# Attention, a gated layer and eight experts in one kernel: steps in pairs over three batches, loads in a set order, routing in one run

## The chip, the cores and the metric

One core of one Trainium2 chip. A core has five engines that run side by side and meet at semaphores: TensorE (PE, matmuls), VectorE (DVE), ScalarE (ACT), GpSimd (POOL) and SyncE (SP, which here issues loads and stores). Transfers run on 16 DMA engines. The metric is the device time of one execution in microseconds (us).

## The reference, cut to what matters

```python
# attention: 4 batches, 8 heads, 576 positions, head size 64; float32
scores = q @ k.T / 8                      # heads 0-3: the last 32 positions
scores = where(mask, scores, -1e9)        # heads 4-7: every 32nd position
x = softmax(scores) @ v                   # -> x: 2304 tokens x 512
x = ((x @ w_a) * (x @ w_b)) @ w_out       # w_*: float64, 512 x 1536 and 1536 x 512
logits = x @ w_gate + log1p(exp(x @ w_noise)) * noise
top2 = the two largest of 8 logits; weights = their softmax
for e in range(8):                        # w1[e]: 512 x 1024, w2[e]: 1024 x 512
    out[tokens of e] += weight * (relu(x @ w1[e]) @ w2[e])
```

## The kernel before

Every product of the two layers is made of three fp32r matmuls (`mm3`, lines 186 to 188), high part by high part, high by low, low by high. So every weight and every activation is split into a high part (written by ACT) and a low part (DVE).

**The stages.** `load_m1` reads the float64 weights as pairs of integers in blocks (`raw`, line 158) and turns them into high and low parts with integer work on DVE and two copies on ACT (`split64`, lines 161 to 177; `ct` is its scratch). It is a generator: `conv_to(n)` runs it up to step n. Attention is worked out in units of two heads of a batch (`Unit`), four units a batch in the order `HPS`. A unit has 14 steps on PE: `T` transposes q and k (4 steps, line 247), `Q` makes scores (2 halves x 2 steps, line 277) and ends in `E`, the softmax on DVE and ACT, `P` transposes the probabilities (4 steps, line 318), `PV` multiplies by v (2 steps, line 331; result in `xf`). `att_pipe` puts the steps of neighbouring units into one another and yields after each.

Batch 0 goes first, alone, with the mask added by a matmul (`pemask`, line 268), and its probabilities come from one exponential for each block of columns (line 306). The main loop then takes five chunks c of tokens (four of 512; the last, of 256, holds the 64 last tokens of each batch, taken from `tails`) through 12 blocks f of the hidden layer each: `stage_a(c, f)` makes a * b for 128 hidden columns (`pa`, `pb`, `gh`, `gl`), and `stage_b` adds the block before to the output (`po`). Between halves of these products `point()` is called, six times a block: it advances one step of attention of batch c + 1 (`attq`), and every third time (every second in the last chunk) one step of what is in `bgq`. There stand, taken in turn: `finish(c)` (router logits of a chunk, then `route`: two best experts, their ranks by a matmul at line 470, the slots, and scatters of (token, weight) into `table`, line 496), `clear_out`, the loads of the first expert (`load_expert`) and `fetch` (line 716 loads 128-row tiles of the table, line 722 gathers their rows, `spread` transposes and splits them, lines 731 to 733). In batches 1 to 3 DVE adds the mask while it reads the scores (line 286); batches 2 and 3 use one wide exponential (`wide`).

The experts follow in passes; there `pump()` advances the same queue.

**What sets the order.** Within the main loop PE runs its instructions in the order in which the program writes them (`tc.manual_schedule`). All other engines, PE before and after that loop, and the DMA queue of SP take what a scheduler with modelled durations puts next, earlier lines first. Every engine runs its own list in order: an instruction that waits holds those behind it.

**Places.** q, k and v tiles of batch 0 rotate through six slots, two of which are the staging slots `st0` and `st1`, which batch 1's `ql` and `kl` and later the experts' weights use. Raw blocks have two buffers, and at step k block k + 1 is asked for:

```python
while len(raws) < min(k + 2, len(blocks), 99 if k >= NPAIR else NPAIR):
    raws.append(load_raw(blocks[len(raws)][0], 512 * blocks[len(raws)][2]))
```

Attention steps and router steps in the main loop use two PSUM buffers with the tag `t`, in turn.

Of the kernel before, what the change touches and what calls it, by code (L numbers as in the profile page):

```python
# [32 lines left out]
def attention_moe_kernel(ctx: ExitStack, tc: tile.TileContext, q, k, v, w_a, w_b, w_out,  # L33
# [165 lines left out]
    class Unit:  # L199
# [4 lines left out]
        def __init__(self, tile, bank, b, hp, pemask, wide):  # L204
            self.tile, self.bank, self.b, self.hp, self.pemask, self.wide = tile, bank, b, hp, pemask, wide
# [30 lines left out]
        def T(self, i):  # L236
# [11 lines left out]
            if self.wide and i // 2:  # L248
# [8 lines left out]
        def Q(self, half, x):  # L257
            n, g, m = self.n, self.g, self.m
            msk = maskAB[:, half:half + 3, :] if self.local else maskS[:, None, :].to_broadcast([72, 4, 72])
            if x == 0:  # L260
                self.s[half] = self.tile("s", [n, 2, g, m])
                st = self.tile("sst", [96, 1 if self.wide else 2, 8])
                self.mx, self.sm[half] = st[:n, 0, 0:2 * g], st[:n, 0 if self.wide else 1, 0:2 * g]
# [3 lines left out]
            if self.pemask:  # L267
                nc.tensor.matmul(ps, identb[:n, :n], msk, start=True, stop=False)
            for ii in range(g):
# [4 lines left out]
                else:  # L274
# [3 lines left out]
                                 start=not self.pemask, stop=not self.pemask or ii == g - 1)  # L278
# [12 lines left out]
        def E(self, half):  # L291
            n, g = self.n, self.g
# [3 lines left out]
            if not self.pemask:  # L296
                nc.vector.tensor_reduce(mx, s3, axis=AX.X, op=OP.max)
            if self.wide:
                if not self.pemask:
# [40 lines left out]
    def att_pipe(us, ahead, done=None):  # L340
# [8 lines left out]
        if ahead == 2:  # L349
            us[1].load_v()  # L350
        for n, u in enumerate(us):
# [11 lines left out]
            if last:  # L363
                last.PV(1)
                if done:
                    done(last)
                if n + ahead - 1 < len(us):
                    us[n + ahead - 1].load_v()
# [22 lines left out]
        if done:  # L391
            done(u)
# [38 lines left out]
    def route(c, lg):  # L431
# [7 lines left out]
        yield  # L439
# [14 lines left out]
        yield  # L454
# [10 lines left out]
        nc.vector.tensor_add(ms, oh[:, :, 0, :], oh[:, :, 1, :])  # L465
        yield
# [26 lines left out]
        yield  # L493
        for j in range(J):
# [7 lines left out]
            yield  # L502

    pair = [None]

    def store_x2(c, ps, j):
        if j % 2 == 0:
            pair[0] = rpool.tile([128, 2, DM], F32, name="row", tag=f"row{j // 2}")
        row = pair[0][:, j % 2, :]
# [13 lines left out]
    bgq, attq = [], []  # L523
# [10 lines left out]
    def pump():  # L534
        advance(attq)
        advance(bgq)

    def drain():
        while bgq or attq:
# [22 lines left out]
    def load_m1():  # L562
# [8 lines left out]
        raws = []  # L571
        for k, (_, f, n, i) in enumerate(blocks):
            while len(raws) < min(k + 2, len(blocks), 99 if k >= NPAIR else NPAIR):
                raws.append(load_raw(blocks[len(raws)][0], 512 * blocks[len(raws)][2]))
# [5 lines left out]
    cp = m1.enter_context(tc.tile_pool(name="conv", bufs=1))  # L580
    a1 = ExitStack()
    p1 = a1.enter_context(tc.tile_pool(name="att1", bufs=1, reuse_waits="tile"))
    nraw = [0]

    def next_of(n):
        nraw[0] += 1
        return nraw[0] % n

    conv_room["raw"] = lambda m: cp.tile([128, 1024, 2], I32, name="raw", tag=f"u{next_of(2)}")[:, 0:m, :]
    cts = []  # L590

    def ct_tile(m):

        if not cts:
            ct = cp.tile([128, 2, 1024], I32, name="ct", tag="u2")
            cts.extend((ct[:, 0], ct[:, 1]))
        cts.append(cts.pop(0))
        return cts[-1][:, 0:m]

    conv_room["ct"] = ct_tile  # L600
    conv = load_m1()
    nconv = [0]
# [9 lines left out]
    def p1tile(name, shape):  # L612
        if name in ("ql", "kl", "vl"):
            nslot[0] += 1
            i = nslot[0] % 6
            return stage.tile(shape, F32, name=name, tag=f"st{i}") if i < 2 else \
                p1.tile(shape, F32, name=name, tag=f"qkv{i}")
        return p1.tile(shape, F32, name=name, tag=name, bufs=P1BUFS[name])

# [15 lines left out]
    att = ExitStack()  # L635
    apool = att.enter_context(tc.tile_pool(name="att", bufs=1, side="right", reuse_waits="tile"))
# [7 lines left out]
    def attend(b, wide):  # L644
        us = [Unit(atile, bank1, b, hp, False, wide) for hp in HPS]
        us[0].load_qk()
        us[0].load_v()
        return att_pipe(us, 1)

    attq.append(attend(1, False))  # L650

    def stage_a(c, f, point):
# [4 lines left out]
        def half(tag, w):  # L657
            ps = psum.tile([128, n], F32, name="pa" if tag == "A" else "pb", tag=tag)
            for i, kd in enumerate(HPS):
                mm3(ps, tuple(t[:, kd, cols] for t in w), xT[c, kd], i == 0, i == KD - 1)  # L660
                if i == 1:
                    point()
# [16 lines left out]
    def stage_b(c, f, g, point):  # L679
# [4 lines left out]
        for j in range(J):  # L684
            mm3(po[c][j], tuple(t[:, 128 * j:128 * j + 128] for t in g), w, f == 0, f == NF - 1)
            if 2 * (j + 1) in (J, 2 * J):
                point()
# [15 lines left out]
    xpool = {}  # L703

    def xset(e, g):
        n = 3 if g == 0 else 2
        p = xpool[e % 2, g]
        if (e, g) not in XS:
            t = f"x{g}{e % 2}"
            XS[e, g] = (p.tile([128, KD, 128 * n], F32R, name=t + "h", tag=t + "h"),  # L710
# [9 lines left out]
    def gather(e, t):  # L720
        g = xpool["g"].tile([128, DM], F32, name="g", tag="g", bufs=2)
# [13 lines left out]
    def fetch(e, tiles):  # L735
# [3 lines left out]
        for t in tiles:  # L739
            gs.append((t, gather(e, t)))  # L740
            yield
            if len(gs) == 2:
# [232 lines left out]
```

## Time and profile before

| | us |
|---|---|
| runs | 1170.78, 1167.08, 1170.57; median 1170.57 |
| the profiled execution | 1169.36 |
| its span, first to last instruction | 1167.6 |
| PE busy | 1102.8 (94%) |
| DVE busy | 525.3 (45%) |
| ACT busy | 418.0 (36%) |
| GpSimd busy | 144.0 (12%) |

Shares are of the span. The main loop's first full block starts at about 85 us, the last chunk at 599 us and the first expert's matmuls at 677 us. Matmuls overlap, so spacing between starts tells more of PE's pace than the length of one.

### The profile page before, as it was taken

To read this page: it belongs to the slowest core of one execution; us is meant where nothing else is said; L and a number is where in the kernel's file an instruction comes from. 1 tells how busy PE (TensorE), PEld (TensorE's weight loads), DVE (VectorE), ACT (ScalarE), POOL (GpSimd) and SP (SyncE) were. 2 spreads that over 40 slices of the span, in tenths; PEclk is the share of its full clock that TensorE was granted. 3 is DMA by queue.
4 is the path that set the end of the run, shared out by engine and by line. 5 is a ranking of instruction groups with operands and counts; after the bars stand their busy time and mean duration, and the time that the engine had idled before them with its cause. 6 is when DMAs were issued, how large, how long until landed. Compare 5 with 4: busy or idle time off the path is not lost.

```text
span 1167.6 us, 16084 instructions
## 1 busy us (share of the span) xinstructions
PE 1102.8 (94%) x6381; PEld 927.2 (79%) x6381; DVE 525.3 (45%) x1109; ACT 418.0 (36%) x936; POOL 144.0 (12%) x136
## 2 busy tenths in 40 slices
PE   6768999999999999999999699999999998999996
PEld 5546777777777777888888589988999897988995
DVE  5688985355435465211326361245342434242111
ACT  5666664233223242221225251244242424232111
POOL 0000000000200002000020313231030313021112
PEclk9969999999999999999999999999999999999998
DMA  8544522101111111730013643266253626242023
GB/s 183 176 123 153 177 80 65 61 22 32 37 26 58 31 36 49 268 112 1 1 37 110 127 126 57 46 194 183 78 139 92 156 82 166 66 116 40 11 35 48
DMA packets 88549, 105.02 MB, mean 90 GB/s; under 512 B 43664, under 2 KB 48400, under 8 KB 88464
## 3 DMA queue, kind: packets, MB, share of 16 engines
q1 hardware_dynamic: 78352, 82.89, 23.9%
q0 software_dynamic: 10112, 21.02, 9.9%
q8 instruction: 52, 0.85, 0.3%
q14 instruction: 33, 0.27, 0.1%
HBM read 78.53 MB, written 25.35 MB: 89 GB/s over the span
## 4 chain that ended last, share of the span: by engine, by line
PE 78%; DMA 10%; DVE 7%; issue 2%; POOL 2%; ACT 1%; SPq 1%; DVEq 0%; ACTq 0%; POOLq 0%
PE ph L186 6%; PE ph L187 6%; PE ph L188 6%; PE py L186 6%; PE py L187 6%; PE py L188 5%; PE po L186 4%; PE pb L186 4%; PE pa L186 4%; PE pb L188 4%; PE pb L187 4%; PE po L188 4%; PE po L187 4%; PE pa L187 4%; PE pa L188 4%; DMA st<-in_moe_w_dram 3%
## 5 line engine op out<-in xcount | busy, mean ns | idle before, releaser
L825 DVE SCALAR_TENSOR_TENSOR hl<-ph,hh 128x256 fp32r<-128x256 f32 (+1 forms) x128 | 62.1, 488 | 198.2 <-ACT hh L824 197.9
L824 ACT ACTIVATE hh<-ph 128x256 fp32r<-128x256 f32 (+1 forms) x128 | 55.2, 433 | 208.5 <-PE ph L188 208.5
L671 DVE TENSOR_TENSOR a<-a,pb 128x512 f32<-128x512 f32 (+1 forms) x60 | 37.9, 631 | 129.2 <-PE pb L188 129.2
L496 POOL DMA_INDIRECT table<-pay,sli x36 | 35.7, 992 | 452.7 <-DVE sli L483 424.3
L849 POOL DMA_INDIRECT out_dram<-y,tb x40 | 65.1, 1627 | 193.1 <-ACT y L848 127.0
L666 ACT ACTIVATE a<-pa 128x512 f32<-128x512 f32 (+1 forms) x60 | 33.2, 553 | 110.0 <-PE pa L188 107.5
L672 ACT ACTIVATE gh<-a 128x512 fp32r<-128x512 f32 (+1 forms) x60 | 35.3, 588 | 81.2 <-DVE a L671 80.2
L722 POOL DMA_INDIRECT g<-x,tb x40 | 40.6, 1016 | 183.1 <-PE tt L731 165.4
L673 DVE TENSOR_TENSOR gl<-a,gh 128x512 fp32r<-128x512 f32 (+1 forms) x60 | 38.0, 633 | 16.3 <-ACT gh L672 15.8
L277 PEld LDWEIGHTS tt<-kT,qT 64*72 64x72 f32 (+1 forms) x336 | 30.4, 149 | 18.2 <-issue 14.9
L318 PE MATMUL tt<-ident,s 72*72 72x72 f32 (+1 forms) x224 | 30.9, 263 | 11.9 <-DVE s L310 7.8
L318 PEld LDWEIGHTS tt<-ident,s 72*72 72x72 f32 (+1 forms) x224 | 24.4, 141 | 22.4 <-ACT ct L168 4.5
L319 ACT ACTIVATE pT<-tt 128x288 f32<-128x288 f32 (+1 forms) x64 | 25.8, 409 | 42.0 <-PE tt L318 41.6
L277 PE MATMUL tt<-kT,qT 64*72 64x72 f32 (+1 forms) x336 | 39.1, 253 | 0.7 <-DVE s L286 0.7
L186 PE MATMUL py<-w6h,hh 128*128 128x512 f32 x80 | 33.1, 416 | 6.8 <-ACT hh L824 3.6
L331 PEld LDWEIGHTS tt<-pT,vl 72*64 72x64 f32 (+1 forms) x448 | 22.3, 156 | 18.6 <-issue 8.6
L331 PE MATMUL tt<-pT,vl 72*64 72x72 f32 (+1 forms) x448 | 29.8, 270 | 5.6 <-ACT pT L319 5.6
L731 PE MATMUL tt<-ident,g 128*128 128x128 f32 x160 | 26.0, 281 | 9.5 <-DMA g<-x,tb 8.1
L186 PE MATMUL py<-w2h,hh 128*128 128x512 f32 x80 | 33.2, 415 | 0.6 <-DVE y L846 0.6
L186 PE MATMUL pa<-xh,w0h 128*128 128x512 f32 (+1 forms) x80 | 33.6, 420 | 0.0
L731 PEld LDWEIGHTS tt<-ident,g 128*128 128x128 f32 x160 | 20.6, 145 | 15.1 <-DMA g<-x,tb 7.6
L187 PE MATMUL py<-w6l,hh 128*128 128x512 f32 x80 | 32.6, 407 | 0.0
(288 smaller groups left out, 3307.8 us busy)
## 6 DMA issues: line engine op xcount, KB each, us to landing
st<-in_moe_w_dram SPq DMA_DIRECT2D x64, 512.0 KB
out_dram<-zero SPq DMA_DIRECT2D x13, 512.0 KB
raw<-in_moe_w_a_dram SPq DMA_DIRECT2D x4, 1024.0 KB
raw<-in_moe_w_b_dram SPq DMA_DIRECT2D x4, 1024.0 KB
raw<-in_moe_w_out_dram SPq DMA_DIRECT2D x4, 1024.0 KB
x<-row SPq DMA_DIRECT2D x16, 256.0 KB
vl<-in_v_dram SPq DMA_DIRECT2D x16, 160.0 KB
ql<-in_q_dram SPq DMA_DIRECT2D x16, 144.0 KB
```

Of the source, the lines that this page charges most:

```text
L186: nc.tensor.matmul(ps, w[0], x[0], start=start, stop=False)
L187: nc.tensor.matmul(ps, w[0], x[1], start=False, stop=False)
L188: nc.tensor.matmul(ps, w[1], x[0], start=False, stop=stop)
L277: nc.tensor.matmul(ps[:, ii, :], self.qT[r0:r0 + 64, q0:q0 + n], self.kT[r0:r0 + 64, k0:k0 + m], start=not self.pemask, stop=not self.pema ...
L318: nc.tensor.transpose(ps[:, ii, :], self.s[half][:, x, ii, :], ident[:n, :n])
L331: nc.tensor.matmul(ps[64 * hh:64 * hh + 64, jl, :], self.vl[:, hh, g * half + jl, :], self.pT[:, x, ii, :], start=True, stop=True)
L673: nc.vector.tensor_sub(gl, a, gh.bitcast(F32))
L722: nc.gpsimd.indirect_dma_start(out=g, out_offset=None, in_=x2, in_offset=bass.IndirectOffsetOnAxis(ap=TB[e, t][:, 0:1], axis=0))
L731: nc.tensor.transpose(ps[:, kd, :], g[:, 128 * kd:128 * kd + 128], ident)
L824: nc.scalar.activation(hh, ph, AF.Relu)
L825: nc.vector.scalar_tensor_tensor(hl, ph, 0.0, hh.bitcast(F32), op0=OP.max, op1=OP.subtract)
L849: ins = nc.gpsimd.indirect_dma_start(out=out, out_offset=bass.IndirectOffsetOnAxis(ap=TB[e, t][:, 0:1], axis=0), in_=y, in_offset=None, co ...
```

## The change

- **Batch 0.** All loads of q, k, v are issued first, unit by unit, with the first three raw blocks between them, and SP runs this part in program order. The tiles lie in places of `ring` that weights of block 4 on will use. Raw blocks have three buffers (the third is the place of `row`), and at step k block k + 2 is asked for. In the second half of units 1 to 3 (`wides`) DVE subtracts the maximum from all columns, ACT makes one exponential, DVE the sum.
- **Batches 1 to 3** are one `att_pipe` of 12 units. `may` holds the first `PV` of a batch until the chunk before has given its `xf` places back. In batch 1 (`mask` is "act") PE adds the mask by matmul, as in batch 0, and ACT copies the scores to SBUF.
- **Points.** Three a block instead of six: after `pa`, after `pb`, after `stage_b`. Each advances attention by a step, then `finq` (now the queue of `finish`) or, if that is empty, attention by a second step, then `bgq`, twice in the last chunk.
- **Routing.** `route` runs without a break up to the one-hot sums, gives way three times, then runs from the rank matmul to all scatters.
- **The first fetch** leaves the queue: table and two gathers ahead of block 8 of the last chunk, first `spread` and third gather ahead of block 11, the rest after the last block. `load_expert(0)` starts at block 4, not 5.
- **Experts.** `fetch` gathers three tiles ahead instead of two; the split rows of one set lie in the place of `row`; a chunk's four rows share one tile.

```diff
             if x == 0:
...
             ps = self.bank("Q", [n, g, m])
-            if self.pemask:
+            pemask = self.mask != "dve"
+            if pemask:
                 nc.tensor.matmul(ps, identb[:n, :n], msk, start=True, stop=False)
...
-            if self.pemask:
+            if self.mask == "pe":
                 nc.vector.tensor_reduce(mx, ps, axis=AX.X, op=OP.max)
-                if self.wide:
+                if self.wides[half]:
                     nc.vector.tensor_sub(s[:, x], ps, mx[:, :, None].to_broadcast([n, g, m]))
                 self.src.append(ps)
             else:
-                nc.vector.tensor_add(s[:, x], ps, msk)
+                if pemask:
+                    nc.scalar.activation(s[:, x], ps, AF.Copy)
+                else:
+                    nc.vector.tensor_add(s[:, x], ps, msk)
                 self.src.append(s[:, x])
...
             if nxt and n + 1 + ahead < len(us):
                 us[n + 1 + ahead].load_qk()
+            while not may(u):
+                yield
             u.PV(0)
             yield
...
     def pump():
-        advance(attq)
+        advance(finq)
         advance(bgq)
...
         for k, (_, f, n, i) in enumerate(blocks):
-            while len(raws) < min(k + 2, len(blocks), 99 if k >= NPAIR else NPAIR):
-                raws.append(load_raw(blocks[len(raws)][0], 512 * blocks[len(raws)][2]))
+            ahead(min(k + (3 if k < NPAIR - 2 else 2), 99 if k >= NPAIR else NPAIR))
...
-    us = [Unit(p1tile, bank0, 0, hp, True, False) for hp in HPS]
-    us[0].load_qk()
-    us[1].load_qk()
-    us[0].load_v()
-    for i, _ in enumerate(att_pipe(us, 2, lambda u: split_kd(0, u.hp))):
-        conv_to(min(12, 1 + i * 12 // 50))
-    conv_to(12)
+    us = [Unit(p1tile, bank0, 0, hp, "pe", (False, i > 0)) for i, hp in enumerate(HPS)]
+    with tc.manual_schedule(engines={mybir.EngineType.SP}):
+        for i, u in enumerate(us):
+            u.load_qk()
+            u.load_v()
+            conv_room["ahead"](min(i + 1, 3))
+        for i, _ in enumerate(att_pipe(us, 9, lambda u: split_kd(0, u.hp))):
+            conv_to(min(12, i * 12 // 50))
+        conv_to(12)
...
-    attq.append(attend(1, False))
+    us = [Unit(atile, bank1, b, hp, "act" if b == 1 else "dve", (b > 1,) * 2) for b in range(1, B) for hp in HPS]
+    us[0].load_qk()
+    us[0].load_v()
+    attended = set()
+    may = [1]
+    attq.append(att_pipe(us, 1, lambda u: attended.add((u.b, u.hp)), lambda u: u.b <= may[0]))
...
             def point():
                 npt[0] += 1
                 if c == 0:
-                    conv_to(n0 + (n1 - n0) * ((npt[0] - 1) % 6 + 1) // 6)
+                    conv_to(n0 + (n1 - n0) * ((npt[0] - 1) % 3 + 1) // 3)
                 advance(attq)
-                if npt[0] % (2 if c == NCH - 1 else 3) == 0:
+                advance(finq if finq else attq)
+                advance(bgq)
+                if c == NCH - 1:
                     advance(bgq)
...
-            if (c, f) == (NCH - 1, 5):
+            if (c, f) == (NCH - 1, 4):
                 bgq.append(load_expert(0))
-            if (c, f) == (NCH - 1, 8):
-                bgq.append(fetch(0, [0, 1, 2]))
+            if c == NCH - 1 and f in (8, 11):
+                for _ in range(3 if f == 8 else 2):
+                    next(first)
```

## Rows read from the trace of the kernel before

**Rows 1.** Busy time by window: us, each engine's busy time (count), granted clock, DMA, GB/s.

```profile
5.00:84.00 79.00, 57.91 (x358) 41.99 (x358) 57.23 (x116) 51.01 (x177) 0.00 (x0) 0.91 0.61 159
84.00:180.00 96.00, 91.82 (x524) 70.10 (x525) 83.83 (x133) 58.70 (x151) 0.00 (x0) 0.95 0.48 143
660.00:677.00 17.00, 8.90 (x49) 7.51 (x48) 3.68 (x8) 3.79 (x8) 6.59 (x7) 0.80 0.50 82
```

**Rows 2.** Waits, 0 to 120 us: waiter, releaser, us in total, times, longest.

```profile
ACT ct L168 <- DVE ct L167: 14.5, 9, 4.6
...
PE tt L318 <- DVE s L310: 7.8, 3, 4.1
...
PE tt L331 <- ACT pT L319: 5.6, 5, 2.2
...
PE tt L247 <- DMA ql<-in_q_dram: 3.8, 1, 3.8
...
PE tt L318 <- ACT xf L334: 3.2, 2, 3.0
```

**Rows 3.** Line 158, the raw loads: who waited for them, us and times.

```profile
  DVE ct L167: 19.1, 14
```

**Rows 4.** SyncE's queue, timeline: start, us, instruction.

```profile
80.31 1.26 SPq L218 DMA_DIRECT2D ql<-in_q_dram  x2
```

**Rows 5.** Waits, 596 to 680 us, the last chunk.

```profile
PE tt L731 <- DMA g<-x,tb: 8.1, 2, 7.4
...
DVE pay L486 <- DMA table<-pay,sli: 3.7, 1, 3.7
...
PE tt L426 <- DVE x2T L420: 2.9, 2, 2.1
...
PE po L186 <- ACT gh L672: 1.6, 1, 1.6
```

**Rows 6.** GpSimd, timeline, with the idle time before and its releaser.

```profile
648.82 0.97 POOL L496 DMA_INDIRECT table<-pay,sli  x1 [0.30 <-issue]
659.46 1.28 POOL L496 DMA_INDIRECT table<-pay,sli  x1 [9.67 <-issue]
```

**Rows 7.** SyncE's queue around 655 us.

```profile
655.58 0.34 SPq L716 DMA_DIRECT2D tb<-table  x1
```

**Rows 8.** DVE by line and shape, 0 to 480 us: busy us, mean ns | idle before.

```profile
L286 DVE TENSOR_TENSOR s<-tt,maskAB 96x384 f32<-96x384 f32 x24 | 13.2, 552 | 9.7 <-PE tt L277 9.3
...
L302 DVE TENSOR_REDUCE sst<-s 96x6 f32<-96x768 f32 x8 | 7.6, 947 | 3.1 <-ACT s L301 3.1
```

**Rows 9.** PE, timeline: start us, duration us, instructions.

```profile
8.11 1.17 PE L268 MATMUL sc<-maskAB,identb 96*96 96x384 bf16 x3
...
49.29 0.63 PE L187 MATMUL pa<-xl,w0h 128*128 128x512 f32 x1
49.72 0.63 PE L188 MATMUL pa<-xh,w0l 128*128 128x512 f32 x1
50.14 1.16 PE L247 MATMUL sc<-ident,ql 72*128 72x72 f32 x8
...
103.10 0.42 PE L247 MATMUL tt<-ident,ql 72*128 72x72 f32 x4
103.32 0.48 PE L186 MATMUL po<-w2h,gh 128*128 128x512 f32 x1
103.64 0.39 PE L187 MATMUL po<-w2l,gh 128*128 128x512 f32 x1
103.86 0.39 PE L188 MATMUL po<-w2h,gl 128*128 128x512 f32 x1
```

**Rows 10.** Transfers of the slot table, then of gathered rows.

```profile
DMA to landing us min/median/max: 2.8/3.6/6.7
...
DMA to landing us min/median/max: 3.3/3.4/7.6
```

**Rows 11.** PE's waits among the experts, 676 to 1140 us.

```profile
PE py L186 <- ACT hh L824: 3.6, 1, 3.6
```

More of the change, by code (lines that the diff above doesn't have):

```diff
@@ L199, in attention_moe_kernel, with __init__ @@
     class Unit:
-        def __init__(self, tile, bank, b, hp, pemask, wide):
-            self.tile, self.bank, self.b, self.hp, self.pemask, self.wide = tile, bank, b, hp, pemask, wide
+        def __init__(self, tile, bank, b, hp, mask, wide):
+            self.tile, self.bank, self.b, self.hp, self.mask, self.wides = tile, bank, b, hp, mask, wide
             self.local = hp < 2
@@ L261, in Q @@
                 self.s[half] = self.tile("s", [n, 2, g, m])
-                st = self.tile("sst", [96, 1 if self.wide else 2, 8])
-                self.mx, self.sm[half] = st[:n, 0, 0:2 * g], st[:n, 0 if self.wide else 1, 0:2 * g]
+                wide = self.wides[half]
+                st = self.tile("sst", [96, 2, 8])
+                self.mx, self.sm[half] = st[:n, 0, 0:2 * g], st[:n, 1, 0:2 * g]
                 self.src = []
@@ L291, in E @@
         def E(self, half):
+            wide = self.wides[half]
             n, g = self.n, self.g
@@ L364, in att_pipe @@
                 last.PV(1)
[L365 to L368, printed above, removed]
+                done(last)
+                if ahead == 1:
+                    u.load_v()
                 yield
@@ L501, in route @@
                 scatters.append(ins)
-            yield
-    pair = [None]
+        yield
+    four = [None]
     def store_x2(c, ps, j):
-        if j % 2 == 0:
-            pair[0] = rpool.tile([128, 2, DM], F32, name="row", tag=f"row{j // 2}")
-        row = pair[0][:, j % 2, :]
+        if j == 0:
+            four[0] = rpool.tile([128, 4, DM], F32, name="row", tag="row")
+        row = four[0][:, j, :]
         if j % 2:
@@ L534, in pump @@
     def pump():
-        advance(attq)
+        advance(finq)
         advance(bgq)
     def drain():
-        while bgq or attq:
+        while bgq or finq:
             pump()
@@ L580, in attention_moe_kernel, with raw_tile, halves, get @@
     cp = m1.enter_context(tc.tile_pool(name="conv", bufs=1))
+    att = ExitStack()
+    apool = att.enter_context(tc.tile_pool(name="att", bufs=1, side="right"))
     a1 = ExitStack()
-    p1 = a1.enter_context(tc.tile_pool(name="att1", bufs=1, reuse_waits="tile"))
+    p1 = a1.enter_context(tc.tile_pool(name="att1", bufs=1))
     nraw = [0]
-    def next_of(n):
+    def raw_tile(m):
         nraw[0] += 1
[L587 to L600, printed above, removed]
+        i = nraw[0] % 3
+        return (cp if i else rpool).tile([128, 1024, 2], I32, name="raw", tag=("row", "u0", "u1")[i])[:, 0:m, :]
+    def halves(pool, shape, name, tag):
+        t = []
+        def get(m):
+            if not t:
+                both = pool.tile([shape[0], 2] + shape[1:], I32, name=name, tag=tag)
+                t.extend((both[:, 0], both[:, 1]))
+            t.append(t.pop(0))
+            return t[-1][:, 0:m]
+        return get
+    conv_room["raw"] = raw_tile
+    conv_room["ct"] = halves(cp, [128, 1024], "ct", "u2")
     conv = load_m1()
+    next(conv)
     nconv = [0]
@@ L613, in p1tile, with slot8 @@
         if name in ("ql", "kl", "vl"):
+            i = nslot[0]
             nslot[0] += 1
-            i = nslot[0] % 6
-            return stage.tile(shape, F32, name=name, tag=f"st{i}") if i < 2 else \
-                p1.tile(shape, F32, name=name, tag=f"qkv{i}")
+            return slot8(i, shape)
         return p1.tile(shape, F32, name=name, tag=name, bufs=P1BUFS[name])
+    big = {}
+    def slot8(i, shape):
+        if i // 2 not in big:
+            big[i // 2] = ring.tile([128, 2, 1024], F32, name=f"qkv{i // 2}", tag=f"w{3 + i // 4}{'hl'[i // 2 % 2]}")
+        n = shape[1] * shape[2] * shape[3]
+        return big[i // 2][:shape[0], i % 2, 0:n].rearrange("p (a b c) -> p a b c", a=shape[1], b=shape[2])
     def bank0(name, shape):
@@ L709, in xset @@
             t = f"x{g}{e % 2}"
+            if p is rpool:
+                both = p.tile([128, 2, KD, 128 * n], F32R, name=t, tag="row")
+                XS[e, g] = (both[:, 0], both[:, 1])
+                return XS[e, g]
             XS[e, g] = (p.tile([128, KD, 128 * n], F32R, name=t + "h", tag=t + "h"),
@@ L749, in attention_moe_kernel @@
     with tc.manual_schedule(engines={mybir.EngineType.PE}):
+        first = fetch(0, [0, 1, 2])
         prev = None
@@ L765, in attention_moe_kernel @@
                 last_units(cp, 10, ("u0", "u1", "u2"))
-                conv_room["raw"] = lambda m: rpool.tile([128, 512, 2], I32, name="raw", tag=f"row{next_of(2)}")
+                conv_room["raw"] = halves(rpool, [128, 512, 2], "raw", "row")
                 conv_room["ct"] = lambda m: rpool.tile([128, 512], I32, name="ct", tag="x2T")
             if f == NF - 1:
-                while attq:
+                while c + 1 < B and (c + 1, HPS[-1]) not in attended:
                     advance(attq)
@@ L801, in attention_moe_kernel @@
         last_rows = stage_b(*prev, pump)
+        for _ in first:
+            pass
     m1.close()
```

60 lines of the change are left out of this document (27 added, 33 removed).

## Prediction, made before the changed kernel was run

> **What bounds the kernel now.** I read the page first: TensorE (PE) is busy nearly everywhere, so time can come only from stretches where it waits, or from its own work. The busy time by window shows where. From 5 to 84 us PE works 57.9 of 79 us and from 84 to 180 us 91.8 of 96; around 660 us it works 8.9 of 17 us at a mean granted clock of 0.80 [rows 1]. Between these stretches the slices of the page are full. So I asked three lists of waits: the start, the last chunk, the experts.
>
> At the start nearly all waits are short ones on ScalarE (ACT), VectorE (DVE) or a load: 5.6 us for `pT`, 7.8 us for `s` (4.1 of it one wait at 110 us, in batch 1), 3.8 us for one load of `ql`, 3.2 us behind `xf` [rows 2]. Two things feed them. DVE sits at the head of its queue for raw weight blocks that have not landed, 19.1 us in 14 waits over the kernel [rows 3], and a softmax step behind it waits too. And the `ql` of batch 1 is issued only at 80.31 us [rows 4], because its place is held by a tile of batch 0.
>
> In the last chunk PE waits 8.1 us for gathered rows, 2.9 us for `x2T`, 1.6 us for `gh` [rows 5]. The gather is late for this reason: scatter 4 of 8 goes out at 648.82 us, then GpSimd stands 9.67 us before scatter 5 [rows 6], while the table load is issued at 655.58 us [rows 7]. The table load was put between the scatters, waits for the first four to land, and the last four wait for it. The 2.9 us have another origin in the same place: DVE stands 3.7 us at `pay` until scatters of the routing before have landed [rows 5].
>
> **The change part by part.** The sum is made against the profiled execution, 1169.36 us (span 1167.6), which is 1.2 us under the median of 1170.57.
>
> *Batch 0's loads first, three raw buffers.* All q, k, v of batch 0 and three raw blocks go out in order, batch 0 no longer uses the staging slots, and a raw block has two conversions of time to land instead of one. PE's idle time from 5 to 84 us is 79 - 57.9 = 21.1 us [rows 1]; that all of it goes is the upper bound. The least is the 3.8 us of `ql`. I take: 3.8 for `ql`; 3.3 of `s` (7.8 less the 4.1 of batch 1, rounded down); and half of the 5.6 + 3.2 that end on ACT, since the last unit's chain from scores to output has no work to hide behind. That is 3.8 + 3.3 + 4.4 = 11.5 us gained, between 3.8 and 21.1. SP is now in program order there: a raw load that waits for its buffer holds the stores of `tails` and later raw loads. Neither has a reader before chunk 0 is under way.
>
> *One exponential per half unit in batch 0 (second halves, three units).* It takes six or eight small exponentials off ACT and gives DVE two subtractions, read from PSUM as the 552 ns addition is, and a sum of at most 947 ns [rows 8]: at most 2.05 us a unit, 6.2 in all. DVE has 79 - 57.2 = 21.8 us free in that window [rows 1]. Cost 0; without that cover 6.2.
>
> *Batch 1's mask on PE, scores copied by ACT.* PE gets 16 more matmuls. Three such took 1.17 us at the start [rows 9], 0.39 each at the lower clock level; half of that at the upper: 3.1 to 6.2 us. Chunk 0 runs at the upper level, and I take 3.5 lost. DVE loses 16 additions of at most 552 ns [rows 8], 8.8 us, in the window where it is busy 83.8 of 96 us; ACT takes the copies and is busy 58.7 [rows 1]. No row shows that copy. By the Trainium skill (ScalarE: Activation LUTs, What ACT_TABLE_LOAD costs) an activation with constant operands costs 186 ns + 0.833 ns per element, which gives an estimate of 0.43 to 0.51 us each and 7.5 us on ACT.
>
> *Steps in pairs.* After an attention step the first big matmul takes 0.32 us to the next start (103.32 to 103.64) and the following one 0.22 [rows 9]: 0.10 per change of kind. Three batches have 3 x 56 steps; pairs save 84 changes at most, 8.4 us. The least is 0: the second step of a pair is itself a change. No row shows two attention steps together at the upper level, so I take 0.03 each, 2.5 gained. The two PSUM buffers come round as before: two steps on. That one pipeline runs over three batches moves steps of a batch into the end of the chunk before and adds none: 0.
>
> *Routing in one run, first in the queue; the fetch at set places.* Routing of chunk 2 now ends in chunk 3, so `pay` is free and the 2.9 us go. All eight scatters precede the table load. In the last chunk routing has 12 steps, three a stage from f = 1, so its rank matmul stands at the end of f = 4, six stages before the first `spread` at f = 11. A stage is 24 matmuls of 256 and 6 of 512 columns; with 0.22 us per 512 [rows 9] that is 4.0 us, 24 in all. Against it: 8 x 1.27 of scatters (0.97 + 0.30) [rows 6], 3.6 to 6.7 to land [rows 10], 3.9 for the table (655.58 to 659.46) [rows 6, 7], 1 of issue and 3.4 to 7.6 for a gather [rows 10]: 22 to 29, and before them some small DVE steps to the slots, which I bound by 0 and 2. So of the 8.1 us, 0 to 7 come back; I take 3, and in it the third gather, issued only when the first `spread` has freed a buffer, with 24 matmuls of 256 and 12 of 512 columns, 5.3 us, to cover it. On GpSimd nothing stands ahead of the gathers but the scatters; on SP the table load stands among the first expert's eight loads, which start a stage earlier (f = 4) with their 16 copies on ACT and 16 subtractions on DVE; PE meets those as before, through `gh`. Routing in one run puts the rank matmul three points behind its input; 1 us for that (0 to 3). The lost clock after the wait, 17 us at 0.80 of which PE worked 8.9 [rows 1], gives back 1. The 1.6 behind `gh` stays. Gained: 8.1 + 2.9 + 1 - 3 - 1 = 8.0, between 2 and 13.6.
>
> *Three gather buffers for the experts, other pools.* The longest PE wait there is 3.6 us [rows 11], behind ACT; it will fall elsewhere. 0, within 7 either way. The rows of x2 now share one buffer of four; the next writer comes a chunk later, and in the experts a pass later: 0. The 4.1 us wait of batch 1 stays: its softmax still has three points of room. It could vanish or double.
>
> **Sum:** -11.5 + 3.5 - 2.5 - 8.0 = -18.5; 1169.4 - 18.5 = **1151 us**, which I give for the median too. Its own range is 1142 to 1160: the half widths of the terms (8.6, 1.5, 4.2, 5.8, 7), halved again and taken as independent, are 6.6, and I add a little for what has no row.
>
> **Clock, row against rule.** At 49.29 and 49.72 us, 512 columns are 0.43 us apart [rows 9], 1.2 GHz, though the window's mean granted clock reads 0.91 [rows 1]; after 103 us they are 0.22 apart, 2.4 GHz. I keep the start at the lower level. The Trainium skill (TensorE: Matmul & The Clock Gate, part 1) says the lower level is the resting state and activity lifts it. By that rule a start with fewer waits would run at the upper level, which is rival C below.
>
> **Rivals.**
>
> A, *conversion takes over.* PE reaches chunk 0 earlier and finds weights not yet split: DVE is busy 83.8 of 96 us there [rows 1]. What the start gains comes back as waits on weights: 1151 + 11.5 = 1163. Against it: 19.1 us of DVE's idle time are the very raw waits that a third buffer covers [rows 3], and DVE loses 8.8 us of additions.
>
> B, *the gather stays late.* Eight landings instead of four, and weight loads on the same DMA engines: 7 us come back instead of 3, the third gather adds 2: 1157.
>
> C, *the start runs at the upper clock.* Two transpose steps together took 1.16 us at 50.14 us, while one at 103.10 us is through in 0.22 [rows 9]: 0.36 a step at most, 32 such steps in batch 0, 11 us more: 1140. Against it: the spacing at 49 us, late in a stretch with few gaps.
>
> D, *slower: ACT becomes the gate of batch 1.* PE now finds each score bank released by ACT, whose queue also holds the conversion steps that wait for DVE: 14.5 us in nine waits up to 120 us, longest 4.6 [rows 2]. A pair has 12 matmuls of 0.22, 2.6 us, of cover. Batch 1 has 28 pairs. If each waits 0.66 us the gain is gone; at the mean of those waits, 1.6 us, 45 are lost: 1196. Against it: transposes already leave through ACT in that queue, and PE is busy 91.8 of 96 us [rows 1].
>
> **How the numbers follow.** My forecast 0.60, A 0.13, B 0.09, C 0.08, D 0.10. Less than 0.3% (3.5 us) cannot be told from no change here. The forecast, B, C and more than half of A are faster: 0.84; the slow end of A is the same: 0.06; D is slower: 0.10. The range leaves out D and the outer half of C, and reaches over A's middle: 1137 to 1165.
>
> **What would show it.** PE idle from 5 us to the first full stage falls from 21 to about 10, and the first stage starts near 73 instead of 84 us; DVE's waits on raw blocks shrink to a few us; no wait on `ql`. In chunk 0 no wait on `w` tiles (else A), and no row of PE waiting for ACT's copy of scores (else D). In the last chunk eight scatters stand together, `pay` waits for nothing, and the first expert's matmuls start about 8 us earlier against the start of that chunk. Wrong would be: full windows up to 660 us that are longer than before, or a gather wait of 7 us.

## The result, and the profile after

| | before | after |
|---|---|---|
| median of 4 runs each, us | 1170.67 (1167.08 to 1172.71) | 1155.24 (1154.18 to 1155.77) |
| profiled span | 1167.6 | 1152.4 |

The ratio is 0.986, 95% interval 0.983 to 0.990: faster. 1151 was forecast with a range of 1137 to 1165, so the total lay in the range. Its terms did not hold. Read at two marks, the first matmul of the last chunk (256 columns wide) and the first matmul of the first expert (`ph`), the span divides so:

| stretch, us | before | after | moved | forecast |
|---|---|---|---|---|
| up to the last chunk | 599.0 | 596.3 | -2.7 | -11.5 + 3.5 - 2.5 = -10.5 |
| last chunk to first expert | 77.6 | 72.0 | -5.6 | -8.0 |
| first expert to the end | 491.0 | 484.0 | -7.0 | 0 |

A gain that was not counted made up for most of two that did not come, so the total was right by luck. Everything below is about these three rows.

Busy time by window, as [rows 1] (PE, its weight loads, DVE, ACT, GpSimd, granted clock, DMA, GB/s):

```profile
5.00:84.00 79.00, 61.76 (x374) 45.88 (x375) 56.15 (x113) 46.26 (x137) 0.00 (x0) 1.00 0.64 153
84.00:180.00 96.00, 89.75 (x528) 70.02 (x526) 83.14 (x128) 62.98 (x165) 0.00 (x0) 0.95 0.49 150
660.00:677.00 17.00, 14.69 (x84) 13.23 (x83) 11.52 (x22) 9.38 (x19) 3.78 (x4) 0.90 0.78 232
```

PE is idle 17.2 us of the first window, not 21.1, and about 10 was forecast. From 84 to 180 us it works less than before. The list of waits from 0 to 120 us says where, against [rows 2]:

```profile
PE sc L247 <- DMA qkv<-in_q_dram: 10.8, 1, 10.8
...
PE tt L324 <- DVE sst L314: 6.2, 1, 6.2
```

The first matmul now waits 10.8 us for its first load (5.2 before). The wait of batch 1's softmax, 4.1 before, is 6.2. The waits on raw blocks are down from 19.1 us [rows 3] to

```profile
  DVE ct L167: 8.0, 5
```

and no wait on `ql` is left. SP's queue seems to show why the start is late (the experiments will say otherwise): seven loads of batch 1 from `ql` on, and one of `wg`, stand ahead of batch 0's `qkv`, which is issued at 5.97 us. The first full stage of chunk 0 starts at 79.0 us; 73 was forecast.

```profile
0.76 1.40 SPq L218 DMA_DIRECT2D ql<-in_q_dram  x2
...
5.97 1.25 SPq L218 DMA_DIRECT2D qkv<-in_q_dram  x2
```

In the last chunk, PE's timeline: the rank matmul waits 6.9 us for `ms`; further on, the first expert waits 2.2 us. The matmuls of 256 columns behind the long wait are 0.21 us apart, where 0.11 to 0.13 is the rule from 635 us on.

```profile
630.98 0.19 PE L474 MATMUL tt<-ms,tri 128*128 128x8 bf16 x1 [6.94 <-DVE ms L467]
...
632.37 0.41 PE L187 MATMUL pa<-xl,w3h 128*128 128x256 f32 x1
632.58 0.41 PE L188 MATMUL pa<-xh,w3l 128*128 128x256 f32 x1
...
668.36 0.61 PE L186 MATMUL ph<-x00h,w0h 128*128 128x384 f32 x2 [2.17 <-ACT x00h L756]
```

The queues that make `ms`, DVE's rows and then one of ACT's: steps of the routing (`t`) stand between the splits of the first expert's weights (`w1l`), and two loads of ACT's table lie on the way, of which the first is shown.

```profile
622.66 0.69 DVE L150 TENSOR_TENSOR w1l<-st,w1h 128x512 fp32r<-128x512 f32 x1 [1.24 <-ACT w1h L149]
...
624.99 0.19 DVE L448 TENSOR_TENSOR t<-t 128x32 f32<-128x32 f32 x1 [0.60 <-ACT t L444]
...
630.74 0.18 DVE L467 TENSOR_TENSOR ms<-oh 128x32 bf16<-128x32 f32 x1
```

```profile
623.43 1.28 ACT L444 ACT_TABLE_LOAD   x1
```

GpSimd's timeline answers to [rows 6]: eight scatters in a row from 634.01 to 643.9, the table behind them, two gathers by 652 us, and the third when the first `spread` has freed its buffer. The 8.1 us wait on a gather [rows 5] is gone.

```profile
634.01 0.97 POOL L499 DMA_INDIRECT table<-pay,sli  x1 [84.20 <-DVE sli L487]
...
650.17 0.98 POOL L746 DMA_INDIRECT g<-x,tb  x1 [6.29 <-issue]
...
659.68 0.95 POOL L746 DMA_INDIRECT g<-x,tb  x1 [7.26 <-PE tt L755]
```

DVE's wait at `pay` (line 490) in the last chunk was forecast to go. It moved to the end of chunk 3, near 552 us. Two more stood in chunks 1 and 2 before the change, too, near 321 and 456 us; the first of them, before, and the total after:

```profile
321.12 0.24 DVE L486 COPY pay<-ids 128x4 int32<-128x4 int32 x2 [3.83 <-DMA table<-pay,sli]
```

```profile
  DMA table<-pay,sli: 13.8, 3
```

The three took 9.5 us before. After, they stand near 300, 436 and 552 us. Before, PE waited 0.7 us near the first and not at all near the second; now it waits 0.85 us at 303 us and 1.1 at 439, and in other kernels with the same code there up to 2.9 and 2.8. PE's waits behind the first expert's matmuls, against [rows 11], where there were four of 8.8 us in all:

```profile
PE py L186 <- ACT hh L855: 2.4, 1, 2.4
PE tt L755 <- ACT y L879: 1.1, 1, 1.1
```

### The profile page after: what moved, and what is told of

Its sections match the earlier page's. It is cut to its first block, busy times and chain, and to the rows that moved or that the text cites. A ratio compares the mean times of both kernels' runs of the same rounds, so it can differ in the third digit from the quotient of the medians.

```text
span 1152.4 us, 16080 instructions
## 1 busy us (share of the span) xinstructions
PE 1096.9 (95%) x6397; PEld 931.6 (81%) x6397; DVE 523.1 (45%) x1099; ACT 414.2 (36%) x911; POOL 142.0 (12%) x136
## 5 line engine op out<-in xcount | busy, mean ns | idle before, releaser
L279 PEld LDWEIGHTS tt<-kT,qT 64*72 64x72 f32 (+1 forms) x336 | 29.5, 149 | 11.9 <-issue 9.8
L186 PE MATMUL pb<-xh,w1h 128*128 128x512 f32 (+1 forms) x80 | 33.0, 413 | 0.0
L187 PE MATMUL pa<-xl,w0h 128*128 128x512 f32 (+1 forms) x80 | 31.1, 389 | 0.8 <-DVE xl L404 0.8
L186 PE MATMUL py<-w3h,hh 128*128 128x512 f32 x80 | 31.8, 398 | 0.0
L186 PE MATMUL pa<-xh,w3h 128*128 128x512 f32 (+1 forms) x80 | 31.7, 396 | 0.0
```

The costliest lines, as they stand in the source:

```text
L186: nc.tensor.matmul(ps, w[0], x[0], start=start, stop=False)
L187: nc.tensor.matmul(ps, w[0], x[1], start=False, stop=False)
L279: nc.tensor.matmul(ps[:, ii, :], self.qT[r0:r0 + 64, q0:q0 + n], self.kT[r0:r0 + 64, k0:k0 + m], start=not pemask, stop=not pemask or ii = ...
```

## The experiments

Twelve kernels, in three groups; each was timed in five rounds against the kernel before on the same chip. That kernel's medians were 1171.4, 1172.3 and 1169.8 us in the three groups. The changed kernel was not timed in them, and its own interval spans 8 us, so a difference of less than some 4 us from it tells nothing. The first theory: the start lost 5 us to loads at the head of SP's queue, the last chunk 6.9 us to the place of the rank matmul, and the experts gained by the third gather buffer. The rival for each: something else sets that time, and the edit moves nothing. Beside the time, the start of each chunk on PE is read (the first `pa` on `w0h`):

| starts, us | chunk 1 | chunk 2 | chunk 3 | last chunk | `ph` | span |
|---|---|---|---|---|---|---|
| before | 220.2 | 357.5 | 494.0 | 599.0 | 676.6 | 1167.6 |
| after | 226.1 | 362.6 | 490.9 | 596.3 | 668.4 | 1152.4 |
| scratch and pay edits | 218.5 | 354.3 | 482.7 | 588.2 | 663.2 | 1149.0 |
| the same, single steps | 225.2 | 365.0 | 494.0 | 599.4 | 673.1 | 1156.4 |

Chunks 1 and 2 can't be set against before directly: the pipeline over three batches does 28 of the 56 transposes of q and k of batch 2, and of batch 3, a chunk earlier. At the start of chunk 3 the same work is done, but for 16 mask matmuls more.

**Batch 1's loads behind batch 0's.**

```diff
         for i, u in enumerate(us):
...
+        us1[0].load_qk()
+        us1[0].load_v()
```

> The changed kernel, with one edit: the first loads of batch 1 (ql, kl, vl) are issued in SP's written order behind batch 0's loads, so they cannot be put ahead of them. Theory (these loads cost the start 5 us: SP issues them from 0.76 to 5.26 us and the first matmul waits until 10.75 instead of 5.16 us): the first matmul at 5.5 to 6.5 us, the first full stage of chunk 0 at 74 instead of 79 us, and the time 1155.2 - 5 = 1150 us. Rival (batch 0 is held by the conversion on DVE or by the raw loads, not by its first load): the first matmul earlier, the first full stage still at 78 to 79 us, and the time 1154 to 1156.

1155.1 us (1150.4 to 1158.4), ratio 0.985 [0.982, 0.987]. The first matmul came at 9.91 us. Now `wg` and the noise had the head of SP's queue:

```profile
0.75 0.44 SPq L106 DMA_DIRECT2D wg<-in_moe_w_gate_dram  x1
...
5.41 1.34 SPq L218 DMA_DIRECT2D qkv<-in_q_dram  x2
```

Batch 0's load was issued at 5.41 us again. The first full stage came at 73.9 us all the same, and chunk 1 at 219.2, 7 us earlier than after; but waits of 2.9 and 2.8 us in chunks 1 and 2 and longer last stretches took it back (its profile is the slowest of its five runs). Neither theory fits the first matmul, and why the first full stage came early behind a late first load stays open. From 5 us to that stage PE is idle 11.1 us, against 16.5 in the changed kernel.

**All of those loads behind.**

```diff
+        us1[0].load_qk()
+        us1[0].load_v()
+        late_loads()                    # wg and noise
```

> The changed kernel with batch 1's first loads and also the loads of wg and of the noise, which took the head of SP's queue in the run that held back batch 1's loads alone, all issued behind batch 0's loads. Theory (the head of SP's queue costs the start 5 us): first matmul at 5.2 to 5.6 us instead of 10.75, first full stage of chunk 0 at 73 to 74 us instead of 79, and the time 1149 to 1151 us. Rival (what the start gains is given back later, in waits that move with it): first full stage at 73 to 74, and the time 1154 to 1156.

1156.7 us (1150.6 to 1159.6), ratio 0.986 [0.983, 0.989]; first matmul at 9.79, first full stage at 79.8 us. Nothing stands ahead of batch 0's first load now, and it is still issued at 5.22 us. The theory of the queue's head fell. SP's own list of waits names the cause, and DVE's timeline its end:

```profile
SPq L220 <- DVE maskAB L81: 4.5, 1, 4.5
```

```profile
4.84 0.29 DVE L81 TENSOR_TENSOR maskAB<-tmp 96x128 bf16<-96x128 f32 x1
```

The first load waits until DVE has written the last mask, 4.84 + 0.29 = 5.13 us. `maskAB` is made from scratch tiles of a pool that is then closed, and the new place of batch 0's q lies in the ring, which begins where that scratch was. The other loads had only gone ahead because they could.

**Two gather buffers.**

```diff
-    GB[0] = 3
+    GB[0] = 2
```

> The changed kernel with two gather buffers in the expert part, as before the change, instead of three. From the first expert's matmul to the end it took 491.0 us before and 484.0 us after. Theory (the third buffer covers the gathers, so the waits behind ACT go): the stretch is 489 to 491 us and the time 1160 to 1162. Rival (the 7 us come from the other order of the last routing and of the loads of expert 1, or from the other pools): the stretch is 484 to 485 us and the time 1154 to 1156.

1163.9 us (1161.0 to 1167.3), ratio 0.994 [0.992, 0.996]: 8.6 us above the changed kernel. But from `ph` to the end its profile shows 488.0 us, 4.0 more than after; the rest was lost earlier, in code that is the same. DVE and PE near 303 us:

```profile
300.63 0.24 DVE L490 COPY pay<-ids 128x4 int32<-128x4 int32 x2 [5.10 <-DMA table<-pay,sli]
```

```profile
303.43 0.74 PE L324 MATMUL tt<-ident,s 96*128 96x96 f32 x3 [2.89 <-ACT qT L251]
```

DVE stands 5.1 us at `pay`, with the softmax steps of batch 2 behind it; ACT waits for these, and PE for ACT's `qT`. PE in the window from 300 to 310 us, here and then in the changed kernel, where the same wait was 0.85 us:

```profile
300.00:310.00 10.00, 7.11 (x28) 0.66 0.14 31
```

```profile
300.00:310.00 10.00, 9.15 (x55) 1.00 0.27 61
```

The granted clock fell to 0.66. Chunk 1 took 141.3 us here and 136.6 in the changed kernel: 2.0 for the longer wait, and 2.7 with the lower clock, at which 512 columns are 0.43 us apart from 305 to 309 us.

**The rank matmul later, by three and by six points.**

```diff
         nc.vector.tensor_add(ms, oh[:, :, 0, :], oh[:, :, 1, :])
         yield
         yield
         yield
+        for _ in range(3 if c == NCH - 2 else 0):      # 6 in the second run
+            yield
```

> The changed kernel with three more points between the routing's softmax and its rank matmul in the last chunk, one stage or 4 us of matmuls. In the changed kernel PE waits 6.9 us there for ms. Theory (PE stands because the order written for PE puts the rank matmul too early, and its input comes at 631 us in any case): the wait falls to 2.5 to 3.5 us and the time by 3 to 4, to 1151 to 1152. Rival (the chain ms, scatters, table, gathers sets when the first expert starts): the wait at ms falls but one at the spread of the gathered rows or at the first expert's matmuls takes its place, and the time stays at 1154 to 1156.

> As the run before, with six more points, 8 us of matmuls. Theory: no wait at ms is left; the spread of the first gathered rows, at its set place, now comes near 652 us while its rows land near 654, so 1 to 2 us come back there: the time falls by 5 to 6, to 1149 to 1150. Rival: 1154 to 1156, with 5 to 7 us of waits at the spread.

1154.6 us (1153.9 to 1156.6), ratio 0.986 [0.984, 0.988], and 1160.4 us (1157.0 to 1164.7), ratio 0.991 [0.989, 0.993]. By three, the wait at `ms` falls from 6.9 to 2.9 us and last chunk to `ph` takes 70.7 us instead of 72.0. By six it is gone, and that stretch takes 76.9. PE's waits in the last chunk of the second, and its scatters and first gather:

```profile
PE tt L757 <- DMA g<-x,tb: 5.2, 1, 5.2
PE po L186 <- ACT gh L694: 3.1, 1, 3.1
```

```profile
637.16 1.19 POOL L501 DMA_INDIRECT table<-pay,sli  x1 [86.84 <-DVE sli L489]
...
657.68 0.98 POOL L748 DMA_INDIRECT g<-x,tb  x1 [9.39 <-issue]
```

The rival holds: `ms`, scatters, table and gathers are one chain, and PE only chooses where it waits for it. Six points later the scatters begin 3 us later (637.16 for 634.01) and the first gather 7.5 us later.

**Four pay buffers.**

```diff
-        pay = rpool.tile([128, J, 2, 2], I32, name="pay", tag="pay", bufs=2)
+        pay = rpool.tile([128, J, 2, 2], I32, name="pay", tag="pay", bufs=4)
```

> The changed kernel with four pay buffers instead of two, so that DVE need not stand at pay until the scatters of an earlier routing have landed (13.8 us in three waits in the changed kernel, near 300, 440 and 552 us). In the profile of the changed kernel PE waits 0.85 us at 303 us and 1.09 us at 439 us; in four other runs with the same code up to there 1.5 to 2.9 and 2.4 to 2.8 us, and in two of them the granted clock stands at 0.66 and 0.87 for the next 10 us. Theory (those waits are DVE standing at pay): both waits go, no clock is lost there, and the time falls by 2 to 5, to 1150 to 1153 us. Rival (other work holds PE there): the waits stay within 1 us, and the time is 1154 to 1156.

1159.0 us (1155.5 to 1160.6), ratio 0.988 [0.985, 0.990]. Half a hit. The wait at 439 us is gone, but there are five routings, and the `pay` of the last was now taken forward to 302 us:

```profile
302.68 0.24 DVE L490 COPY pay<-ids 128x2 int32<-128x2 int32 x2 [5.96 <-DMA table<-pay,sli]
```

PE then waited 3.8 us at 305 us. By its time the run can't be told from the changed kernel.

**The mask on DVE again.**

```diff
-    us = [Unit(atile, bank1, b, hp, "act" if b == 1 else "dve", (b > 1,) * 2) for b in range(1, B) for hp in HPS]
+    us = [Unit(atile, bank1, b, hp, "dve", (b > 1,) * 2) for b in range(1, B) for hp in HPS]
```

> The changed kernel with batch 1's mask added on DVE again: 16 matmuls fewer on PE, no score copies on ACT, 16 additions more on DVE. Theory (the mask costs PE 3.5 us, and the 6.3 us wait at 110 us is the softmax's steps standing between conversion steps, so it does not depend on the additions): 84 to 180 us shows the wait at 5 to 7 us, and the time is 1151 to 1153. Rival (the additions fill DVE, so the softmax comes later still): the waits from 84 to 180 us grow by 4 or more, and the time is 1156 to 1160.

1166.1 us (1161.8 to 1172.1), ratio 0.995 [0.993, 0.997]: 10.9 above the changed kernel. The rival holds, more than its numbers. In the profile chunk 0, from its first full stage to chunk 1 and the only one that the edit touches, takes 154.4 us instead of 147.1; chunks 1 and 2 lose another 6.7, at longer waits behind `pay` (3.2 us, and 2.2 where after had 1.1) and with a lower clock behind them. PE's waits from 84 to 180 us, where after had one of 6.2:

```profile
PE tt L324 <- DVE sst L314: 8.1, 1, 8.1
PE tt L324 <- ACT gh L692: 7.5, 1, 7.5
```

**Single steps.**

```diff
                 advance(attq)
-                advance(finq if finq else attq)
+                advance(finq)
...
+                if i == 1 and not finq:              # stage_a, half way through pa and pb
+                    advance(attq)
...
+            if 2 * (j + 1) == J and not finq:        # stage_b, half way through po
+                advance(attq)
```

> The changed kernel with attention steps one at a time at six points of a stage instead of two at a time at three, while no routing is under way. Theory (each pair saves a change of kind between matmuls, 0.03 us, 2.5 in all): 1157 to 1159. Rival one (the second step of a pair is itself such a change): 1155 plus or minus 1. Rival two (two steps at once ask more of ACT and DVE than their queues give, and make the 6.3 us wait at 110 us): that wait falls to 4 us or less, and the time is 1152 to 1154.

1154.1 us (1153.4 to 1157.5), ratio 0.984 [0.982, 0.987], no different from after. From 84 to 480 us PE has one listed wait, and those at 303 and 439 us are gone:

```profile
PE tt L324 <- DVE s L316: 5.1, 1, 5.1
```

So two things change at once, and the price of a pair can't be read from the time: chunk 1 took 138.6 us, 2.0 more than after, with the wait of 0.85 us gone.

**Scratch moved, a pay for each routing.**

```diff
-    with tc.tile_pool(name="setup", bufs=1) as sp:
+    with tc.tile_pool(name="setup", bufs=1, side="right") as sp:
-        pay = rpool.tile([128, J, 2, 2], I32, name="pay", tag="pay", bufs=2)
+        pay = rpool.tile([128, J, 2, 2], I32, name="pay", tag="pay", bufs=5)
```

> The changed kernel with two edits. The scratch of the mask setup lies on the other side of the on-chip memory, since the run with the loads in order showed SP's first load waiting 4.5 us for DVE's maskAB: the loads of batch 0 were never held by what was issued ahead of them, but by the scratch whose place their buffer takes. And pay has a buffer for each of the five routings, since with four the last routing's pay still stood 6.0 us. Theory: first matmul at 5.2 to 5.6 us, first full stage of chunk 0 at 73 to 75 us, no PE wait over 0.9 us near 303 and 439 us, no clock lost there, and the time 1155.2 - 5 - 2 = 1148, at most 1150 us. Rival (the gains are given back on the way, as in the two runs that moved the loads): 1153 to 1156, with longer waits in chunk 0 or the last chunk.

1150.0 us (1146.2 to 1150.8), ratio 0.982 [0.979, 0.985]: the fastest here. SP's first row and PE's first:

```profile
0.76 1.41 SPq L218 DMA_DIRECT2D qkv<-in_q_dram  x2
```

```profile
4.74 1.19 PE L247 MATMUL sc<-ident,qkv 96*128 96x96 f32 x6 [4.74 <-DMA qkv<-in_q_dram]
```

PE's two longest waits from 84 to 480 us (the 6.2 is 3.7 here, and nothing waits at 303 or 439):

```profile
PE tt L324 <- DVE s L316: 3.7, 1, 3.7
PE tt L324 <- issue: 0.9, 1, 0.9
```

First full stage at 73.8 us, as expected; from 5 us to it PE is idle 12.3 us. The last chunk starts at 588.2 us, 10.8 earlier than in the kernel before, where 10.5 was forecast. Against the changed kernel 3 us were given back in the last chunk (75.0 us to `ph`) and 1.8 in the experts. The two edits were not timed apart.

**Three variants of that kernel**, on the same chip.

Single steps and two gather buffers are edited as above; one exponential for each half unit of batch 1 is

```diff
-    us = [Unit(atile, bank1, b, hp, "act" if b == 1 else "dve", (b > 1,) * 2) for b in range(1, B) for hp in HPS]
+    us = [Unit(atile, bank1, b, hp, "act" if b == 1 else "dve", (True,) * 2) for b in range(1, B) for hp in HPS]
```

> The kernel with the scratch and pay edits, and attention steps one at a time. With the changed kernel single steps gave 1154.1 against 1155.2 us, but there they also took away the waits at 303 and 439 us; here these are gone in any case. Theory (pairs save 2.5 us of changes between kinds of matmul): 2 to 3 us above the run with the two edits alone. Rival (they save nothing): within 1 us of it or below.

1160.0 us (1157.4 to 1160.7), ratio 0.991 [0.988, 0.994]: 10 above. Chunks 1 and 2 take 268.7 us, in pairs 264.2, with the same counts of attention matmuls in each. Of these 4.5 us, 1.0 is a wait that only this kernel has. Chunk 1 shows it best. Less its one listed wait, it takes 138.6 and 138.8 us in the two kernels with single steps. In pairs it takes 135.7 or 135.8: in the changed kernel, with the rank matmul later, with all loads in order and with the scratch moved. Another 6.7 are lost before chunk 1, where the softmax of batch 1 holds PE longest:

```profile
PE tt L324 <- DVE sst L315: 8.4, 1, 8.4
```

8.4 us, not 3.7; with the scratch in its old place single steps had made that wait shorter (5.1, not 6.2). (In the profile the last chunk starts 11.2 us later; 3.8 come back behind it.)

> The kernel with the scratch and pay edits, and two gather buffers for the experts instead of three. In the first run with two the time was 8.6 us longer, but in its profile only 4.0 of them lay behind the first expert's matmul and the rest came from the clock lost near 303 us, which is the same code. Theory (the third buffer is worth 4 us): 3 to 5 us above the run with the two edits alone, and 487 to 489 us from the first expert's matmul to the end. Rival one (worth 8): 7 to 9 above, 491 to 493. Rival two (nothing): within 1, 483 to 485.

1155.8 us (1154.2 to 1157.0), ratio 0.987 [0.985, 0.990]: 5.8 above, and 491.8 us from `ph` to the end against 485.8. PE waits behind `y` that three buffers don't show:

```profile
PE tt L755 <- ACT y L879: 1.7, 1, 1.7
PE py L186 <- ACT y L879: 1.2, 1, 1.2
PE py L186 <- DVE y L877: 1.0, 1, 1.0
```

With three there is none behind `y`; beside the wait at `hh` that both have (2.5 and 2.6), only

```profile
PE ph L186 <- DVE hl L856: 0.4, 2, 0.2
```

> The kernel with the scratch and pay edits, and in batch 1 one exponential for each half unit instead of six or eight: ACT loses some 2 us a half unit, DVE gets a subtraction and a sum, 0.95 us each. Theory (the 6.3 us wait at 110 us is two softmax halves passing between ACT's small exponentials and DVE's conversion steps): that wait falls to 3 us or less, and the time by 2 to 4 below the run with the two edits alone. Rival (DVE is the fuller queue there, and adding the mask on it cost 11 us): the waits from 84 to 180 us grow, and the time is 3 to 8 above.

1155.6 us (1153.2 to 1160.3), ratio 0.988 [0.985, 0.991]: 5.5 above. The rival holds; from 84 to 180 us:

```profile
PE tt L324 <- DVE sst L315: 9.0, 1, 9.0
```

## Why the prediction was right, and where it was wrong

**The start (-11.5 forecast).** The step that failed is the 11.5 itself, in that it let batch 0's first load go out at once because it stood first. I named who reads the raw loads that SP holds in program order, and did not ask what had lain before in the place where the first load writes. It waits 4.5 us for DVE's masks. (In the sum itself, 7.8 less 4.1 is 3.7 and not 3.3, so the step's own rows give 11.9.) The rest of the step held: no `ql` wait, DVE's raw waits 8.0 instead of 19.1. With the scratch moved, the stretch up to the last chunk is 10.8 us shorter than before, of 10.5 forecast for start, mask and pairs together; in the changed kernel it is 2.7. That 10.8 and 10.5 meet is partly luck: the terms of mask and pairs were mis-sized, as the next two paragraphs show, and the edit to `pay` is in it. Nor is the first load all of the start: with batch 1's loads behind, the first full stage came at 73.9 us behind a first matmul at 9.91 us. PE's order before the main loop differs between these kernels.

**The mask (+3.5).** The 16 matmuls are busy 5.2 us:

```profile
L270 PE MATMUL tt<-maskAB,identb 96*96 96x384 bf16 x8 | 2.8, 345 | 0.0
...
L270 PE MATMUL tt<-maskS,identb 72*72 72x288 bf16 x8 | 2.4, 300 | 0.0
```

0.35 and 0.30 us each, against 0.22 taken, inside the bounds. But taking them out made the kernel 10.9 us slower, 7.3 of it in chunk 0, so the term's sign was wrong in this company: the 8.8 us of additions were called DVE's gain and then put down at nothing. They stand in front of a softmax on which PE waits. The estimate from the Trainium skill (ScalarE: Activation LUTs, What ACT_TABLE_LOAD costs) was 0.43 to 0.51 us for a copy by ACT; this trace shows 0.40 and 0.48, a little less, by ACT's lines,

```profile
L289 ACT ACTIVATE s<-tt 96x384 f32<-96x384 f32 x8 | 3.8, 480 | 1.6 <-PE tt L279 1.6
...
L289 ACT ACTIVATE s<-tt 72x288 f32<-72x288 f32 x8 | 3.2, 403 | 2.0 <-PE tt L279 2.0
```

and no PE wait on them, so rival D did not come.

**Pairs (-2.5).** Chunks 1 and 2 gain 3.5 us by pairs that no listed wait explains (4.5 less 1.0). Of that 3.0 lie in chunk 1, where some 60 steps make 30 pairs at most: about 0.10 us each, an estimate from these counts. So 0.03 us a change was too little, and the upper bound of 0.10 was near. The larger part of the 10 us, in chunk 0, goes with one wait (3.7 or 8.4 us) that is not the price of a pair, since single steps also had it shorter. In the changed kernel pairs and single steps come out even: in pairs PE waits behind DVE's stop at `pay` (0.85 to 2.9 us near 300 us in the kernels with two `pay` buffers and batch 1's mask on PE), in single steps it doesn't.

**The 4.1 us wait of batch 1** was forecast to stay, with the remark that it could vanish or double: it was 6.2, and from 2.8 to 9.0 in the other kernels. Adding DVE work there (mask, subtraction and sum) made it longer both times, the second time with ACT's small exponentials gone, so fewer of these are no cure. DVE's rows ahead of the 6.2 us show what fills it:

```profile
103.48 0.16 DVE L314 TENSOR_SCALAR sst<-sst 96x6 f32<-96x6 f32 x1
105.23 1.22 DVE L170 SCALAR_TENSOR_TENSOR ct<-raw,ct 128x1024 int32<-128x1024 int32 x1 [1.59 <-ACT ct L168]
...
106.97 0.18 DVE L315 RECIPROCAL sst<-sst 96x6 f32<-96x6 f32 x1
...
108.77 0.94 DVE L316 TENSOR_TENSOR s<-s,sst 96x768 f32<-96x768 f32 x1
```

Four conversion steps and 1.59 us of waiting for ACT stand between the softmax's last three steps, so that work of 1.28 us takes 6.2. No run took the conversion steps away alone.

**The last chunk (-8.0, measured -5.6).** The waits on the gather and on `x2T` went, and eight scatters stand together, as forecast. Two steps failed. The rank matmul behind its input was priced at 1 us, at most 3: it waits 6.9. And `pay` waits for something: it only waits elsewhere. The first does not cost its 6.9 us, though: with that wait at 2.9 or gone the time is the same or longer, since `ms` to gathers is one chain. That the chain starts late because the first expert's splits and two table loads stand between its steps is what the rows show; no run took them away.

**The experts (0, measured -7.0).** The third gather buffer was put down at nothing, "it will fall elsewhere". It is worth 5.8 us by the runs with the scratch moved; in the profiles 4.0 and 6.0. The profiles scatter here: from `ph` to the end, kernels with three buffers take 482.6 to 487.4 us, those with two 488.0 and 491.8. The gain lay within the 7 given either way. The total held because 7.0 came here, where none was forecast, while 7.8 and 2.4 were missing in the two stretches before; that is luck.

**The other rivals.** A: no wait on `w` tiles in chunk 0. B: PE waits for a gather only with the rank matmul moved (1.0 and 5.2 us). C: the start still runs at the lower level; at 83.4 us 512 columns are 0.43 us apart, 1.2 GHz, although the granted clock of that window reads 1.00.

Open: why the stretch from last chunk to `ph` takes 72.0 to 75.4 us in kernels with the same code in it, and what sets the clock behind the short waits (below).

## What to carry to other kernels

Before a load is put first, look up what lay in its destination: a first load waits for the last reader of closed scratch (4.5 us here), and SP's own list of waits shows it. A wait that is taken out of one stage is to be looked for in the stages before, at the same line: here the one at `pay` moved a chunk ahead, and two others at that line, which had cost PE 0.7 us in all, now held another batch's softmax. When a total comes out right, divide the span at marks before believing the terms.

## What was not expected of the hardware

A short stop of PE can cost more than itself: behind 2.9 us at 303 us, in the run with two gather buffers, the granted clock from 300 to 310 us read 0.66, behind 0.85 us in the changed kernel 1.00. But behind 2.7 us at 302 us in the run with all loads in order it was 1.00 as well, while behind 2.45 us at 439 us in that run 512 columns were 0.43 us apart from 441 us on, for 3 us. The Trainium skill (TensorE: Matmul & The Clock Gate, part 1) has the lower level as the resting state, and the 0.21 us between matmuls behind the wait at `ms` agrees; no run here tells which stop lowers the clock and which doesn't.

Each of the 11 loads of ACT's table took 1.28 us, two for each routing (for `Ln` and for the next `Exp`). The Trainium skill (ScalarE: Activation LUTs, Table sets: the hidden batching unit) says that one set holds both functions; no run here tried it.
